# Transposed weights and attention output in one two-bank PSUM tile, four PSUM tiles for the val and proj chains

## The chip, the cores and the metric

The kernel runs on 1 core of one Trainium2 chip. Its metric is the device time of one execution in microseconds; the times below are medians of several runs.

## The reference

The reference is three steps in a row on float32 inputs (batch 8, 576 tokens, 8 heads of 64; the weights arrive as float64).

```python
scores = scale * np.matmul(q_c, k_c.transpose(0, 1, 2, 4, 3))   # chunks of 64 tokens
attn = np.exp(scores - max); attn = attn / (sum + 1e-09)
x = np.matmul(attn, v_c)                     # -> (8, 576, 512)

gate_pre[t] = sum over k of conv_w[k] * x[t - 4 + k]     # causal, 5 taps, per channel
x = (sigmoid(gate_pre) * (x @ w_val)) @ w_out

xn = (x - mu) / sqrt(var + 1e-06) * g_ln
out = x + np.maximum(xn @ w_ch1, 0.0) @ w_ch2            # 512 -> 2048 -> 512
```

## The kernel before

The kernel has two parts. The **attention stage**, up to about 344 us of the span, does the attention, the gated convolution and its two products. The **feed-forward stage** fills the rest; it starts with one block of 512 tokens in plain form (`ff1`, `ff2`: `psh`, `acc`) while the weights are still decoded (`split_ff`: VectorE's `da`, GpSimd's `w`), and goes on with pairs of blocks (`ff_pair`: `zy`, `x`, `psf`, `acc`). The change edits the attention stage alone.

The attention stage walks over 18 units of 256 tokens, one to a **slot** (`slot(u)`), and over 9 **blocks** of 512 tokens, two units each. For a unit u:

- `a3(u)`: scores. TensorE writes `sc` (two banks); VectorE takes the maximum (`mx`, line 167) and subtracts it (`ex`, line 170), ScalarE takes the exponential (line 174), VectorE the sum, the reciprocal (`sm`) and the product (`pr`, line 179).
- `a4(u)`, a slot later: eight TensorE transposes of `pr` into `pst` (line 186), which ScalarE copies to `pT` (line 188).
- `a5(u)`: TensorE multiplies `pT` by v into `x` (line 219, two banks). ScalarE copies `x` to `xf` (for the convolution) and rounds it to `xh`; VectorE makes the rest, `xl = x - xh` (line 238).

For a block j, once its two units are there:

- `conv(j, f, ...)`: per feature tile f (four of 128 channels) one ScalarE instruction (line 248) and four on VectorE (line 250), into `cg`; `sigm(j)`: one ScalarE sigmoid over all of `cg` (line 257).
- `val(j, f)`: a chain of 12 matmuls into one bank, `psv`; VectorE multiplies it by the gate (`gv`, line 282), ScalarE rounds that to `gh`, VectorE makes `gl` (line 286).
- `proj(j, t)`: per 128 tokens a chain of 12 matmuls into one bank, `pso`, over all four `gh` and `gl`; ScalarE copies it to `y` and sends it to DRAM (lines 299, 300).

The chains of a block are spread over the slots behind it, so that a slot holds its own `sc`, `pst` and `x` and four chains of earlier blocks. The first four slots are issued on TensorE in the order of the code; from slot 4 on a list scheduler sets the order on every engine by its own estimates and by which buffers it finds free, so another number of PSUM tiles gives another order. VectorE and ScalarE carry some work of the next stage as filling: the decode of the feed-forward weights of the first blocks (`da`, lines 87 to 90).

The eight PSUM banks of the stage go to four pools of two: `ps_s` for `sc`, `ps_x` for `x`, `ps_p` for `pst` (each one tile of two banks), and `ps_d` for the chains (two tiles of one bank). A chain may start when the chain two before it has been read: a `psv` by `gv`, a `pso` by `y`. Only the last block's `psv` have four tiles of their own (`acc`).

Of the kernel before, what the change touches and what calls it, by code (L numbers as in the profile page):

```python
# [8 lines left out]
F32 = mybir.dt.float32  # L9
# [5 lines left out]
PSUM = bass.MemoryType.PSUM  # L15
# [4 lines left out]
def tile_chunk_attention_gated_mlp(ctx: ExitStack, tc: tile.TileContext, qk, v, w_val, conv_w, w_out, g_ln, w1, w2, out):  # L20
    nc = tc.nc
    B, S, DM = out.shape
# [8 lines left out]
    P = 128  # L31
    BLK = 512
# [4 lines left out]
    NP = H // 2  # L37
# [10 lines left out]
    def boundary(j):  # L48
        o = (-(j * BLK)) % S
        return o if 0 < o < BLK else BLK  # L50
# [5 lines left out]
    ps_d = ctx.enter_context(tc.tile_pool(name="ps_d", bufs=2, space=PSUM))  # L56
# [4 lines left out]
    s_a = ExitStack()  # L61
    pA = s_a.enter_context(tc.tile_pool(name="pA", bufs=2, side="right"))
    ps_s = s_a.enter_context(tc.tile_pool(name="ps_s", bufs=1, space=PSUM))
    ps_x = s_a.enter_context(tc.tile_pool(name="ps_x", bufs=1, space=PSUM))
    ps_p = s_a.enter_context(tc.tile_pool(name="ps_p", bufs=1, space=PSUM))

    a_dram = [dram.tile([P, DM], F32, name=f"ad{f}") for f in range(NF)]
    w1c = [dram.tile([P, 2, 2, 2 * P], F32, name=f"wc{i}") for i in range(NF * 7 // 4)]
# [15 lines left out]
    def decode(raw, a):  # L84

        lw, hw, au = raw[:, :, 0], raw[:, :, 1], a.bitcast(U32)
        nc.scalar.activation(out=a, in_=hw.bitcast(F32), func=ACTF.Copy, scale=2.0 ** -112)
        nc.vector.tensor_scalar(out=au, in0=au, scalar1=3, scalar2=None, op0=ALU.logical_shift_left)
        nc.vector.scalar_tensor_tensor(out=au, in0=hw, scalar=0x80000000, in1=au, op0=ALU.bitwise_and, op1=ALU.bitwise_or)  # L89
        nc.vector.scalar_tensor_tensor(out=au, in0=lw, scalar=29, in1=au, op0=ALU.logical_shift_right, op1=ALU.bitwise_or)  # L90
# [55 lines left out]
    NG = NP * UN // P  # L146
# [34 lines left out]
    def a4(u):  # L181
        pr = pt.pop(u)
        t = pA.tile([P, NG, P], F32, tag="pT", name="pT", bufs=1)
        ps = ps_p.tile([P, NG, P], F32, tag="p", name="pst")
        for g in range(NG):
            nc.tensor.transpose(out=ps[:, g, :], in_=pr[:, g].rearrange("p r k -> p (r k)"), identity=ident)
        with tc.high_priority():
            nc.scalar.activation(out=t, in_=ps, func=ACTF.Copy)
            pT[u] = t
# [71 lines left out]
    def chain(ps, ops):  # L261
        n = len(ops)
        for i, (lt, rh) in enumerate(ops):
            nc.tensor.matmul(out=ps, lhsT=lt, rhs=rh, start=(i == 0), stop=(i == n - 1))  # L264

    def val(j, f):
        hs, ls = wv["vs"]
        fs = slice(f * P, (f + 1) * P)
        if j == NB - 1:
            ps = p2["acc"].tile([P, BLK], F32, tag=f"acc{f}", name="psv")  # L270
        else:
            ps = ps_d.tile([P, BLK], F32, tag="d", name="psv")
        ops = []
        for c in range(CT):
            ops += [(hs[c][:, fs], xh[j][:, c, :]), (hs[c][:, fs], xl[j][:, c, :]), (ls[c][:, fs], xh[j][:, c, :])]
        chain(ps, ops)
        o = boundary(j)
        gv = pD2.tile([P, BLK], F32, tag="gv", name="gv")
        with tc.high_priority():
            for lo, hi, sh in ((0, o, 0), (o, BLK, HALO)):  # L280
                if lo < hi:
                    nc.vector.tensor_tensor(out=gv[:, lo:hi], in0=ps[:, lo:hi], in1=cg[:, f, lo + sh:hi + sh], op=ALU.mult)  # L282
            a = pD1.tile([P, BLK], F32R, tag=f"gh{f}", name="gh")
            b = pD1.tile([P, BLK], F32R, tag=f"gl{f}", name="gl")
            nc.scalar.activation(out=a, in_=gv, func=ACTF.Copy)
            nc.vector.tensor_tensor(out=b, in0=gv, in1=a, op=ALU.subtract)  # L286
        gh[j, f], gl[j, f] = a, b

    def proj(j, t):
        hs, ls = wv["os"]  # L290
        ts = slice(t * P, (t + 1) * P)
        ps = ps_d.tile([P, DM], F32, tag="d", name="pso")
        ops = []
        for f in range(CT):
            ops += [(gh[j, f][:, ts], hs[f]), (gh[j, f][:, ts], ls[f]), (gl[j, f][:, ts], hs[f])]
        chain(ps, ops)
        y = pD2.tile([P, DM], F32, tag="y", name="y")
        with tc.high_priority():
            nc.scalar.activation(out=y, in_=ps, func=ACTF.Copy)
            nc.scalar.dma_start(out=y_dram[j][ts, :], in_=y)  # L300
# [4 lines left out]
    p2 = {}  # L305
# [67 lines left out]
    acc = {}  # L373
# [220 lines left out]
    def slot(u):  # L594
        d = [dense.get((u, i), []) for i in range(4)]
        if u + 2 < NU:
            load_qkv(u + 2)
        warm(u, 0)
        if u < NU:
            a3(u)  # L600
        warm(u, 1)
        for fn in d[0]:
            fn()
        if LAG <= u < NU + LAG:
            a4(u - LAG)
        warm(u, 2)
        for fn in d[1]:
            fn()
        if LAG <= u < NU + LAG:
            a5(u - LAG)  # L610
        warm(u, 3)
        for fn in d[2] + d[3]:
            fn()
# [30 lines left out]
    def taps():  # L644
        cwr = stg.tile([KC * CT, P], F32, tag="da", bufs=3, name="cwr")
        decode(cwu, cwr)
        ps = ps_p.tile([P, NP * P], F32, tag="p", name="pst")
        nc.tensor.transpose(out=ps[:, 0:KC * CT], in_=cwr, identity=ident[0:KC * CT, 0:KC * CT])
        nc.tensor.transpose(out=ps[:, KC * CT:(KC + 1) * CT], in_=gr, identity=ident[0:CT, 0:CT])
        nc.vector.tensor_copy(out=cw, in_=ps[:, 0:(KC + 1) * CT])  # L650
# [4 lines left out]

    at(0, 3, lambda: split_w("v"))
    at(1, 0, taps)
    at(1, 3, lambda: load_w(w_out, "o", CT))
    for c in range(CT):
        at([2, 3, 3, 4][c], [3, 0, 3, 0][c], lambda c=c: split_w("o", c, c + 1))  # L660
    for j in range(NB):
        u = UPB * (j + 1) + LAG - 1
        for f in range(CT):
            if j == NB - 1:
                at(u, 1, lambda j=j, f=f: conv(j, f, 0))
                at(u, 3, lambda j=j, f=f: conv(j, f, 1))
            elif j:
                at(*[(u, 3), (u, 3), (u + 1, 1), (u + 1, 1)][f], lambda j=j, f=f: conv(j, f, 2))
            else:
                at(u - 1, 3, lambda j=j, f=f: conv(j, f, 0))  # L670
                at(*[(u, 3), (u, 3), (u + 1, 0), (u + 1, 0)][f], lambda j=j, f=f: conv(j, f, 1))
        if j < NB - 1:
            at(u + 1, 2, lambda j=j: sigm(j))
        for f in range(CT):
            at(*[(u + 1, 2), (u + 1, 3), (u + 2, 0), (u + 2, 1)][f], lambda j=j, f=f: val(j, f))
        for t in range(BLK // P):
            at(*[(u + 2, 2), (u + 2, 3), (u + 3, 0), (u + 3, 1)][t], lambda j=j, t=t: proj(j, t))
# [123 lines left out]
```

## Time and profile before

| | |
|---|---|
| median of 3 runs | 1138.32 us (1137.65 to 1139.07) |
| the profiled execution's own time | 1135.95 us |
| its span in the trace | 1134.2 us, mean granted clock of TensorE 0.977 |
| TensorE busy | 1070.5 us |
| VectorE busy | 712.8 us |
| ScalarE busy | 483.5 us |
| GpSimd busy | 110.6 us |

A busy time is the sum over one engine's instructions. In the rows PE is TensorE's matmuls, PEld its weight loads, DVE VectorE, ACT ScalarE, POOL GpSimd, SP the queue of SyncE that issues the loads. `L264` is line 264 of the kernel before. A timeline row has start, duration, engine, line, operation, output and inputs, count, and in brackets the idle time before it with what ended it. All times are in microseconds, counted from the start of the span.

### The profile page before, as it was taken

To read this page: it belongs to the slowest core of one execution; us is meant where nothing else is said; L and a number is where in the kernel's file an instruction comes from. 1 tells how busy PE (TensorE), PEld (TensorE's weight loads), DVE (VectorE), ACT (ScalarE), POOL (GpSimd) and SP (SyncE) were. 2 spreads that over 40 slices of the span, in tenths; PEclk is the share of its full clock that TensorE was granted. 3 is DMA by queue.
4 is the path that set the end of the run, shared out by engine and by line. 5 is a ranking of instruction groups with operands and counts; after the bars stand their busy time and mean duration, and the time that the engine had idled before them with its cause. 6 is when DMAs were issued, how large, how long until landed. Compare 5 with 4: busy or idle time off the path is not lost.

```text
span 1134.2 us, 17091 instructions
## 1 busy us (share of the span) xinstructions
PE 1070.5 (94%) x6862; PEld 871.4 (77%) x6862; DVE 712.8 (63%) x1171; ACT 483.5 (43%) x832; POOL 110.6 (10%) x120
## 2 busy tenths in 40 slices
PE   5788989899898989899999999999999999999998
PEld 5676767777786868688888888888888888878877
DVE  6999999888967877545647434447444437432434
ACT  3566666566574754434444123333223333221221
POOL 2021001000003443322210000000000000000000
PEclk9799999999999999999999999999999999999999
DMA  8535546531135753634342733332733222622212
GB/s 334 169 121 166 187 133 213 179 107 72 46 120 188 225 165 119 236 118 145 126 141 100 232 99 106 112 106 89 232 105 103 99 93 89 227 93 93 75 38 75
DMA packets 58581, 155.28 MB, mean 137 GB/s; under 512 B 5742, under 2 KB 13958, under 8 KB 56198
## 3 DMA queue, kind: packets, MB, share of 16 engines
q1 hardware_dynamic: 53318, 144.75, 37.7%
q10 hardware_dynamic: 5184, 9.44, 2.2%
q8 instruction: 54, 0.88, 0.3%
q14 instruction: 25, 0.20, 0.1%
HBM read 116.41 MB, written 37.75 MB: 136 GB/s over the span
## 4 chain that ended last, share of the span: by engine, by line
PE 65%; DVE 24%; issue 4%; ACT 3%; DMA 3%; POOL 0%; SPq 0%; ACTq 0%; POOLq 0%; DVEq 0%
PE acc L499 16%; PE x L525 15%; PE psf L499 14%; PE zy L525 10%; DVE cg L250 7%; PE psv L264 5%; DVE da L89 2%; DVE da L90 2%; DVE sm L176 2%; PE acc L385 1%; DVE xl L238 1%; DMA raw<-in_moe_w_ch 1%; DVE h L537 1%; PE psh L264 1%; DVE mx L167 1%
## 5 line engine op out<-in xcount | busy, mean ns | idle before, releaser
L545 DVE TENSOR_TENSOR c<-x,c 128x512 f32<-128x512 f32 x96 | 66.2, 690 | 237.3 <-ACT c L541 181.1
L499 PE MATMUL psf<-w,h 128*128 128x512 f32 x768 | 186.0, 391 | 0.0
L499 PE MATMUL acc<-w,h 128*128 128x512 f32 x768 | 186.0, 391 | 0.0
L499 PEld LDWEIGHTS acc<-w,h 128*128 128x128 f32 x768 | 144.2, 188 | 31.4
L499 PEld LDWEIGHTS psf<-w,h 128*128 128x128 f32 x768 | 144.2, 188 | 31.4
L525 PE MATMUL x<-t,wc 128*128 128x512 f32 x576 | 148.2, 393 | 3.4 <-DVE c L545 3.4
L541 ACT ACTIVATE c<-zy 128x512 f32<-128x512 f32 x96 | 58.0, 604 | 188.4 <-PE zy L525 188.3
L525 PEld LDWEIGHTS x<-t,wc 128*128 128x128 f32 x576 | 108.8, 189 | 27.8 <-DVE c L545 4.6
L536 ACT ACTIVATE h<-c 128x512 fp32r<-128x512 f32 x96 | 60.5, 631 | 136.1 <-DVE c L545 135.5
L250 DVE SCALAR_TENSOR_TENSOR cg<-xf,cw,cg 128x516 f32<-128x516 f32 (+1 forms) x176 | 108.6, 661 | 0.0
L504 DVE TENSOR_TENSOR yt<-psf,yt 128x512 f32<-128x512 f32 x128 | 88.2, 691 | 25.0 <-PE psf L499 21.1
L525 PE MATMUL zy<-b,wc 128*128 128x512 f32 x384 | 98.9, 393 | 0.0
L525 PEld LDWEIGHTS zy<-b,wc 128*128 128x128 f32 x384 | 71.2, 188 | 14.6
L537 DVE SCALAR_TENSOR_TENSOR h<-c,h 128x512 fp32r<-128x512 f32 x96 | 68.5, 713 | 14.0 <-ACT h L536 13.9
L264 PE MATMUL psv<-xh,vh 128*128 128x512 f32 x144 | 62.1, 432 | 15.5 <-DVE gv L282 15.5
L96 POOL TENSOR_TENSOR w<-da,w 128x512 fp32r<-128x512 f32 x32 | 48.6, 1526 | 128.8 <-ACT w L95 125.6
L264 PE MATMUL psv<-xh,vl 128*128 128x512 f32 x144 | 59.6, 414 | 0.0
L264 PE MATMUL psv<-xl,vh 128*128 128x512 f32 x144 | 59.6, 414 | 0.0
L264 PE MATMUL pso<-oh,gh 128*128 128x512 f32 x144 | 58.5, 406 | 0.1
L264 PE MATMUL pso<-oh,gl 128*128 128x512 f32 x144 | 56.5, 393 | 0.4 <-DVE gl L286 0.4
L264 PE MATMUL pso<-ol,gh 128*128 128x512 f32 x144 | 56.1, 390 | 0.0
L393 POOL TENSOR_TENSOR wc<-raws,wc 128x256 fp32r<-128x256 f32 x56 | 45.3, 831 | 107.4 <-ACT wc L392 100.5
(108 smaller groups left out, 1563.3 us busy)
## 6 DMA issues: line engine op xcount, KB each, us to landing
wc<-wc SPq DMA_DIRECT2D x112, 512.0 KB, 3.2
qkr<-in_qk SPq DMA_DIRECT2D x18, 1024.0 KB, 5.9
raw<-in_moe_w_ch SPq DMA_DIRECT2D x32, 512.0 KB, 4.2
vr<-in_v SPq DMA_DIRECT2D x18, 512.0 KB, 4.2
yd<-y ACTq DMA_DIRECT2D x36, 256.0 KB, 2.8
out<-yt SPq DMA_DIRECT2D x36, 256.0 KB, 3.7
yr<-yd SPq DMA_DIRECT2D x32, 256.0 KB, 3.2
yt<-yd SPq DMA_DIRECT2D x32, 256.0 KB, 4.1
```

Source lines behind the costliest of these rows:

```text
L89: nc.vector.scalar_tensor_tensor(out=au, in0=hw, scalar=0x80000000, in1=au, op0=ALU.bitwise_and, op1=ALU.bitwise_or)
L96: nc.gpsimd.tensor_tensor(out=lo, in0=a, in1=hi, op=ALU.subtract)
L250: nc.vector.scalar_tensor_tensor(out=o, in0=x[:, f, i + lo:i + hi], scalar=cw[:, i * CT + f:i * CT + f + 1], in1=o, op0=ALU.mult, op1=ALU.add,
L264: nc.tensor.matmul(out=ps, lhsT=lt, rhs=rh, start=(i == 0), stop=(i == n - 1))
L393: eng.tensor_tensor(out=lo, in0=a, in1=hi, op=ALU.subtract)
L499: nc.tensor.matmul(out=ps, lhsT=lt, rhs=rh, start=(g == 0 and k == 0 and (first or half)), stop=(g == 1 and k == 2 and (last or half)),)
L504: nc.vector.tensor_tensor(out=yt[i], in0=ps, in1=yt[i], op=ALU.add)
L525: nc.tensor.matmul(out=ps, lhsT=lt, rhs=rh, start=(start and c == 0 and i == 0), stop=(c == 1 and i == 2), skip_group_check=True)
L536: nc.scalar.activation(out=t[:, 0, :], in_=src, func=ACTF.Relu)
L537: nc.vector.scalar_tensor_tensor(out=t[:, 1, :], in0=src, scalar=0.0, in1=t[:, 0, :], op0=ALU.max, op1=ALU.subtract)
L541: nc.scalar.activation(out=t, in_=zy, func=ACTF.Copy)
L545: nc.vector.tensor_tensor(out=t, in0=x, in1=t, op=ALU.add)
```

## The change

The pool `ps_p` is gone. The transposes `pst` go into the tile of `ps_x`, tag `x`, which `x` uses too: one tile of two banks that holds `pst` and `x` in turn. The two banks that this frees become the pool `ps_e`, two tiles of one bank, and `val` and `proj` take their tiles from `ps_d` and `ps_e` by turns as long as the stage lasts (`prep` closes it and sets `p2["acc"]`; from there on chains use `ps_d` alone). A small transpose of the convolution's taps moves from `ps_p` to `ps_e`.

```diff
-    ps_p = s_a.enter_context(tc.tile_pool(name="ps_p", bufs=1, space=PSUM))
+    ps_e = s_a.enter_context(tc.tile_pool(name="ps_e", bufs=2, space=PSUM))
...
     def a4(u):
         pr = pt.pop(u)
         t = pA.tile([P, NG, P], F32, tag="pT", name="pT", bufs=1)
-        ps = ps_p.tile([P, NG, P], F32, tag="p", name="pst")
+        ps = ps_x.tile([P, NG, P], F32, tag="x", name="pst")
...
+    chains = 0
+
+    def ps_chain(name):
+        nonlocal chains
+        chains += 1
+        pool = ps_d if chains % 2 or "acc" in p2 else ps_e
+        return pool.tile([P, BLK], F32, tag="d", name=name)
...
         else:
-            ps = ps_d.tile([P, BLK], F32, tag="d", name="psv")
+            ps = ps_chain("psv")
...
-        ps = ps_d.tile([P, DM], F32, tag="d", name="pso")
+        ps = ps_chain("pso")
...
-        ps = ps_p.tile([P, NP * P], F32, tag="p", name="pst")
+        ps = ps_e.tile([P, BLK], F32, tag="d", name="pst")
```

The scheduler gives another order. On TensorE, in the even slots of the stage's second half, where `val` chains run (here around block 5), the order before is this; the rows are the last matmuls of a block's second `psv` chain, `sc`, `pst`, and the start of its third chain:

```order
L264 MATMUL psv<-xl,vh_275 128x512
L264 MATMUL psv<-xh,vl_276 128x512
L162 MATMUL sc<-qkr 64x64 x32
L186 MATMUL pst<-ident,pr 128x128 x8
L264 MATMUL psv<-xh,vh_248 128x512
```

In the change the same place reads:

```order
L264 MATMUL psv<-xl,vh_275 128x512
L264 MATMUL psv<-xh,vl_276 128x512
L162 MATMUL sc<-qkr 64x64 x32
L264 MATMUL psv<-xh,vh_248 128x512
L264 MATMUL psv<-xl,vh_248 128x512
```

The whole third chain has moved ahead of `pst`, and the fourth stands between `pst` and `x`, where before both stood behind `pst` and ahead of `x`. The slots with `proj` chains keep their order (two chains, `sc`, a chain, `pst`, a chain, `x`).

On VectorE, at the end of block 5's convolution, the order before is this (`cg` is the convolution, `gv` the product with the gate):

```order
L179 TENSOR_TENSOR pr<-ex_144,sm 128x1024
L250 SCALAR_TENSOR_TENSOR cg<-xf,cw,cg 128x516
L238 TENSOR_TENSOR xl<-x,xh 128x4x256
L250 SCALAR_TENSOR_TENSOR cg<-xf,cw,cg 128x516
L282 TENSOR_TENSOR gv<-psv,cg 128x320 x2
```

In the change:

```order
L238 TENSOR_TENSOR xl<-x,xh 128x4x256
L250 SCALAR_TENSOR_TENSOR cg<-xf,cw,cg 128x516
L89 SCALAR_TENSOR_TENSOR da<-raw_3785,da 128x512
L250 SCALAR_TENSOR_TENSOR cg<-xf,cw,cg 128x516
L90 SCALAR_TENSOR_TENSOR da<-raw_3785,da 128x512
L88 TENSOR_SCALAR da<-da 128x512
L89 SCALAR_TENSOR_TENSOR da<-raw_3885,da 128x512
L90 SCALAR_TENSOR_TENSOR da<-raw_3885,da 128x512
L167 TENSOR_REDUCE mx<-sc 128x16
L290 TENSOR_TENSOR gv<-psv,cg 128x320 x2
```

Steps of the weights' decode, which before were all done by block 4, now reach into block 5, and `mx` of the next unit has moved ahead of `gv`. Blocks 6 and 7 have no decode steps at this place in either order.

On TensorE in the slot of the last unit, where block 7's chains run, the order before is:

```order
L264 MATMUL psv<-xl,vh_275 128x512
L264 MATMUL psv<-xh,vl_276 128x512
L186 MATMUL pst<-ident,pr 128x128 x8
L219 MATMUL x<-pT,vr 64x64 x9
L264 MATMUL psv<-xh,vh_248 128x512
L264 MATMUL psv<-xl,vh_248 128x512
```

and in the change, from the end of the third chain on:

```order
L264 MATMUL psv<-xl,vh_275 128x512
L264 MATMUL psv<-xh,vl_276 128x512
L186 MATMUL pst<-ident,pr 128x128 x8
L264 MATMUL psv<-xh,vh_248 128x512
L264 MATMUL psv<-xl,vh_248 128x512
```

Before, `pst` and the first part of `x` follow the second chain and chains 3 and 4 come behind; in the change three chains are ahead of `pst`, and the fourth is ahead of `x`.

## Rows read from the trace of the kernel before

**Rows 1.** The page: span, and busy time of each engine.

```profile
span 1134.2 us, 17091 instructions
...
PE 1070.5 (94%) x6862; PEld 871.4 (77%) x6862; DVE 712.8 (63%) x1171; ACT 483.5 (43%) x832; POOL 110.6 (10%) x120
```

**Rows 2.** Windows: stretch, its length, busy time (count) by engine, TensorE's clock, DMA share.

```profile
237.29:270.14 32.85, 30.64 (x368) 24.63 (x368) 27.78 (x41) 19.66 (x26) 0.70 (x1) 0.95 0.35 124
302.38:344.20 41.82, 41.82 (x249) 34.54 (x250) 29.30 (x69) 27.20 (x51) 0.00 (x0) 1.00 0.35 125
344.20:450.00 105.80, 98.05 (x422) 78.38 (x422) 85.48 (x147) 62.00 (x125) 45.16 (x33) 0.97 0.51 165
450.00:1134.20 684.20, 674.31 (x2971) 548.51 (x2969) 328.83 (x557) 215.14 (x422) 36.25 (x48) 1.00 0.36 123
```

**Rows 3.** TensorE's waits from 56 to 344 us: total, times, longest.

```profile
PE psv L264 <- DVE gv L282: 15.5, 6, 5.1
PE x L219 <- ACT pT L188: 9.5, 4, 3.2
```

**Rows 4.** VectorE's waits from 56 to 299.4 us.

```profile
DVE gv L282 <- PE psv L264: 11.3, 9, 2.1
DVE gv L282 <- ACT cg L257: 4.2, 3, 2.0
DVE sm L176 <- ACT ex L174: 2.4, 1, 2.4
```

**Rows 5.** Timeline of VectorE, blocks 5 and 6.

```profile
233.41 1.22 DVE L238 TENSOR_TENSOR xl<-x,xh 128x1024 fp32r<-128x1024 f32 x1
234.55 0.74 DVE L250 SCALAR_TENSOR_TENSOR cg<-xf,cw,cg 128x516 f32<-128x516 f32 x1
237.29 1.42 DVE L282 TENSOR_TENSOR gv<-psv,cg 128x320 f32<-128x320 f32 x4 [1.99 <-ACT cg L257]
...
243.08 0.76 DVE L282 TENSOR_TENSOR gv<-psv,cg 128x320 f32<-128x320 f32 x2 [0.92 <-PE psv L264]
245.97 0.76 DVE L282 TENSOR_TENSOR gv<-psv,cg 128x320 f32<-128x320 f32 x2 [2.13 <-PE psv L264]
...
253.01 0.68 DVE L238 TENSOR_TENSOR xl<-x,xh 128x512 fp32r<-128x512 f32 x1
...
270.14 1.42 DVE L282 TENSOR_TENSOR gv<-psv,cg 128x384 f32<-128x384 f32 x4 [2.00 <-ACT cg L257]
```

**Rows 6.** Timeline of TensorE, block 5.

```profile
227.42 1.16 PE L219 MATMUL x<-pT,vr 64*64 64x64 f32 x64
...
234.18 1.16 PE L162 MATMUL sc<-qkr 64*64 64x64 f32 x64
235.27 1.09 PE L186 MATMUL pst<-ident,pr 128*128 128x128 f32 x8
238.58 0.47 PE L264 MATMUL psv<-xh,vh 128*128 128x512 f32 x1 [2.22 <-DVE gv L282]
...
245.86 1.16 PE L219 MATMUL x<-pT,vr 64*64 64x64 f32 x64
```

**Rows 7.** Timeline of TensorE: the stage's last two chain matmuls.

```profile
343.56 0.39 PE L264 MATMUL pso<-ol,gh 128*128 128x512 f32 x1
343.78 0.39 PE L264 MATMUL pso<-oh,gl 128*128 128x512 f32 x1
```

**Rows 8.** The page's DMA issues: a weight load, with its time to landing.

```profile
raw<-in_moe_w_ch SPq DMA_DIRECT2D x32, 512.0 KB, 4.2
```

**Rows 9.** Groups of instructions to 480 us: busy, mean ns, idle before.

```profile
L87 ACT ACTIVATE da<-raw 128x512 f32<-128x512 f32 x40 | 26.6, 675 | 21.2 <-DMA raw<-in_moe_w_ch 8.8 <-DMA raw<-in_moe_w_val 7.5 <-POOL w L96 2.3
```

**Rows 10.** Timelines of VectorE, TensorE and GpSimd at the stage's end.

```profile
298.71 0.75 DVE L250 SCALAR_TENSOR_TENSOR cg<-xf,cw,cg 128x516 f32<-128x516 f32 x1
...
302.38 0.56 PE L219 MATMUL x<-pT,vr 64*64 64x64 f32 x18 [3.08 <-ACT pT L188]
...
346.31 1.29 POOL L96 TENSOR_TENSOR w<-da,w 128x512 fp32r<-128x512 f32 x1 [65.88 <-ACT w L95]
```

## Prediction

> **What bounds the kernel now.** I read the page's busy shares first, then the waits of each engine, then the timelines of one block of the attention stage on three engines, and last the tail of the stage. The shares [rows 1] show TensorE busy for 94% of the span and VectorE for 63%, which would make TensorE the bound everywhere. Cut into stretches the picture splits. From 450 us to the end TensorE is busy 674.31 of 684.20 us [rows 2]: nothing of this change touches that part, and it can only start sooner or later as a whole. In a block of the attention stage, here 237.29 to 270.14 us, TensorE is busy 30.64 of 32.85 us and VectorE 27.78 [rows 2]: two engines near their limit that wait for each other in turn.
>
> The waits say who waits. Between 56 and 344 us TensorE waits 15.5 us before `psv` for `gv` and 9.5 us before `x` for `pT` [rows 3]. VectorE, up to the last convolution of block 7 at 299.4 us, waits 11.3 us before `gv` for `psv`, 4.2 us before `gv` for the sigmoid (`cg`), and 2.4 us before `sm` [rows 4], with 0.5 us of small ones: 18.5 us in all.
>
> One block shows the ring that these waits form. At 234.55 VectorE does the last convolution instruction; it then waits 1.99 us for ScalarE's sigmoid, and the first two `gv` start at 237.29 [rows 5]. TensorE has finished two `psv` chains by 234.18 and may not start the third, because both chain tiles still hold products that wait for the sigmoid. It does `sc` and `pst` and stands until 238.58 [rows 6]. So VectorE then starves in turn: the third `gv` waits 0.92 us and the fourth 2.13 us for chains that TensorE began too late [rows 5]. Each engine's wait is the other's. TensorE's share of a block is 96 chain matmuls at 0.227 us from start to start [rows 7] and two each of `sc`, `pst` and `x` at 1.16, 1.09 and 1.16 us [rows 6], some 28.6 us at the full clock (its busy time of 30.64 was at a mean clock of 0.95 [rows 2]). So the block takes 32.85 us where neither needs more than about 28.6.
>
> **What the change removes.** With four chain tiles the third and fourth `psv` chain need no `gv`. In the order of the change TensorE does chain 3 right behind `sc`, and chain 4 behind `pst`. With the block's own times: `sc` ends at 235.3, chain 3 (12 x 0.227 = 2.7 us) at 238.0, `pst` at 239.0, chain 4 at 241.7, `x` at 242.9, where it ended at 247.02 before [rows 6, 7]. The third and fourth `gv` would then find their products: VectorE's 0.92 and 2.13 us fall away, and its sequence, whose order in the late blocks is nearly the same, moves up by 3.05 us. `pso` needs the fourth `gl`, which then ends near 246.0, while TensorE reaches `pso` at 242.9 and has some 4 us of products over the first two features to do; so little stands there. VectorE is then the bound, with 27.78 us of work and what it still waits for the sigmoid.
>
> Summed over the stage up to 299.4 us: all of the 11.3 us of `gv` for `psv` goes. One sigmoid wait of 1.99 us goes too, since the decodes of the first feed-forward weights (`da`) now stand between the last convolution and `gv` of block 5, where nothing stood; the wait of block 6 (2.00 us) stays [rows 5]. Of the 2.4 us before `sm`, a single wait early in the stage, I take half. Together 11.3 + 2.0 + 1.2 = 14.5 us.
>
> **What it adds.** First, every `pst` now waits until `x` of the slot before has been read by `xf`, `xh` and, last, by `xl` on VectorE. In the block shown, `xl` ends 6.05 us after `x` in the even slot (228.58 to 234.63) and 6.67 us in the odd one (247.02 to 253.69) [rows 5, 6]. Between that `x` and the next `pst`, TensorE has two chains, `sc` and a third chain to do: 5.45 + 1.16 + 2.7 = 9.3 us [rows 6, 7]. So the wait is covered by 2.6 us; with `x` 4.1 us earlier and `xl` 3.05 us earlier, by 1.5 us. If the cover is gone, TensorE stands for the excess with `pso` queued behind it, and at first only `pT` and the next `x` are late, which VectorE needs half a slot later. I cost it at nothing, with 0 to 4 us as bounds. The Trainium skill speaks against this edit: Perfetto Trace Analysis, section Optimizing Tensor Performance, wants independent matmul groups to rotate through different PSUM banks, so that the evacuation of one overlaps the next group; transposes and outputs lose that here, the chains gain it. By that rule, for the transposes alone, the sum would be that of rival 4 below, 1152 us; by the rows it is nothing, since the next group has 9.3 us of other products ahead of it.
>
> Second, block 4's decodes run later: a weight load must wait for VectorE's decode of the previous tile, and ScalarE's first step of the next decode stands in its queue ahead of two `gh`. The load takes 4.2 us to land [rows 8], then comes 0.7 us of ScalarE [rows 9] and then `gh`; VectorE has some 5 us of other work meanwhile (an estimate from the order: `mx`, four pieces of `gv`, `ex` and three decode steps). That leaves 0.7 to 1.6 us, with 0 to 4 as bounds; I take 2. Third, two engines that run this close will find small new waits; nothing before shows them. Bounds: 0, and 0.8 us a block (30.64, if TensorE's clock stays at 0.95, less 29.8 for VectorE) for eight blocks, 6.4 us. I take 1. Net up to 299.4 us: 14.5 - 2 - 1 = 11.5 us.
>
> **The tail.** From 302.38 to 344.20 us TensorE works without a gap [rows 2], so there it is the bound, and it counts how far TensorE has come when VectorE ends block 7's convolution. Before, when that convolution ends at 298.71 + 0.75, it stands; it waits 3.08 us for `pT`, which ScalarE does only after the sigmoid, up to 302.38 [rows 10], and has all of chains 3 and 4 ahead. In the change both lie before `x`. Followed through, block 7's `pso` would end about 19.5 us after the convolution instead of 21.0; then `psv` and `pso` of block 8 follow, where `gv` and `gl` come a little after the chains. I take 2.0 us more, with 0 and 5.5 us (two chains) as bounds.
>
> What follows is tied to that end: GpSimd's first `w` after the stage starts at 346.31 [rows 10], right after the last `pso` at 343.78 [rows 7], so the stretch up to 450 us moves with it, and so does the rest.
>
> **Sum.** 11.5 + 2.0 = 13.5 us. The profiled execution took 1135.95 us (span 1134.2), which gives 1122.5; the median of the runs shown, 1138.32, is 2.4 us above it, so 1138.3 - 13.5 = 1124.8 us.
>
> **The rivals.**
> 1. *The gain is half lost* (TensorE's clock stays at 0.95, or `pst` waits for `xl`, or ScalarE's queue holds `gh` back). For it: both engines need 28 to 30 us of a block, and ScalarE does `xf`, `xh` ahead of the last `gh` in the early blocks. Against it: without the stalls there is less reason for the clock to fall. It gives 13.5 - 6.4 = 7, so 1131 us.
> 2. *More is gained*: also the other sigmoid wait, all of `sm` and the full 5.5 us of the tail, and none of the new waits: 11.3 + 4.0 + 2.4 + 5.5 = 23, so 1115 us. Against it: nothing fills block 6's sigmoid wait in the new order.
> 3. *No change*: the next stage starts at its old time because its weight loads or normalisation pace it. For it: VectorE is busy 85.48 of 105.80 us there [rows 2]. Against it: `w` waits for the stage's end. 1138 us.
> 4. *Slower*: the shared tile becomes a loop of its own. It is `x` read out (6.67 us), `pst` (1.0), a chain (2.7, over `pT`), `x` (1.16), 11.6 us from one `x` to the next. A slot takes 16.4 us now. It decides once `xl` comes 4.9 us later behind `x` than now, which takes about eight convolution instructions (5.3 us) of VectorE ahead of it. Each further us costs 14 us over the 14 slots; with one, 1152 us. (The Trainium skill's rule on banks, Perfetto Trace Analysis, Optimizing Tensor Performance, points this way.) Against it: in the new order `xl` stands beside `pr`, ahead of most of them.
>
> **How the numbers follow.** Chances: forecast 0.58, rival 1 0.20, rival 2 0.10, no change 0.06, slower 0.06. The likeliest gives 1124.8, its own range 1119 to 1129. To hold 8 in 10 the range goes to 1116 (most of rival 2 left out) and 1133 (most of rival 1 taken in). About 0.2%, 2.3 us, is what a measurement of this kernel can tell from no change; faster by more holds 0.58 + 0.20 + 0.10 less a little for the weak end of rival 1: 0.87. Same 0.07, slower 0.06.
>
> **What the profile after would show.** Right: TensorE's 15.5 us before `psv` for `gv` gone or under 2; VectorE's `gv` for `psv` under 2; a block in 29.5 to 30.5 us; `x` without the waits for `pT` late in the stage; the last `pso` near 330 us, and the time from there to the end within 2 us of before. Wrong: `pst` with a wait for `xl` in most slots, `pso` waiting for `gl` by as much as `psv` did for `gv`, or a shift that is gone by 450 us.

## The result, and the profile after

The change takes 1123.63 us (median of 4 runs, 1120.93 to 1124.58) where before takes 1137.99 (median of 4 runs, 1134.46 to 1139.07): a ratio of 0.9875, 95% interval 0.9847 to 0.9903. That is 14.4 us less; the forecast was 13.5 less, 1124.8 us. The profiled execution took 1124.26 us. One run of experiment 4 below took 1319.74 us at a granted clock of 0.749, where its others had 0.98; it is left out of that row. The page of the change, beside [rows 1]:

```profile
span 1122.4 us, 17077 instructions
...
PE 1069.3 (95%) x6862; PEld 866.7 (77%) x6862; DVE 715.7 (64%) x1171; ACT 482.0 (43%) x832; POOL 108.8 (10%) x120
```

The work is the same, VectorE's even longer by 2.9 us; what went is idle time. The waits of the attention stage say which. (Line numbers in a run's rows are those of its own kernel: `gv` is line 282 before, 290 in the change, 283 in experiment 9.) TensorE after (from 56 to 344 us; total, times, longest), to be held against [rows 3]:

```profile
PE pso L264 <- DVE gl L294: 6.7, 6, 2.2
PE pso L264 <- ACT gh L293: 5.4, 6, 1.5
PE x L219 <- ACT pT L188: 0.9, 1, 0.9
```

VectorE after (56 to 300 us), to be held against [rows 4]:

```profile
DVE gv L290 <- ACT cg L257: 4.0, 2, 2.0
DVE sm L176 <- ACT ex L174: 2.3, 4, 0.7
```

`psv` no longer waits for `gv`, nor `gv` for `psv`: the ring of [rows 5, 6] is gone on both sides. No `pst` waits for `xl`. New are 12.1 us of TensorE before `pso`, for `gl` and `gh`; none of that reaches VectorE, whose list holds nothing but the sigmoid's and `sm`'s waits.

To see what this was worth, cut both traces at the same instruction, the first `gv` of block 7. Windows, before, then after (columns as in [rows 2]):

```profile
56.00:301.45 245.45, 220.54 (x2612) 176.81 (x2608) 224.78 (x334) 154.53 (x201) 21.31 (x24) 0.95 0.42 140
```

```profile
56.00:290.46 234.46, 222.51 (x2620) 175.17 (x2620) 227.85 (x333) 152.72 (x199) 19.74 (x24) 0.97 0.43 147
...
230.92:260.08 29.16, 27.52 (x357) 21.62 (x356) 26.55 (x42) 19.20 (x25) 0.46 (x1) 1.00 0.50 174
260.08:290.46 30.38, 29.48 (x316) 23.58 (x315) 27.68 (x42) 19.25 (x25) 0.32 (x1) 1.00 0.10 36
```

The stretch is 11.0 us shorter. (The work up to this mark is not quite the same: 334 and 333 VectorE instructions, 2612 and 2620 matmuls.) VectorE's idle time in it fell from 245.45 - 224.78 = 20.7 to 234.46 - 227.85 = 6.6 us, 14.1 less, and its busy time rose by 3.1. Two of the remaining waits, 4.0 of the 6.6 us, are the sigmoid's. In VectorE's timeline they stand before the first `gv` of blocks 6 and 7, and where the first feed-forward weights' decodes fill the place, in block 5, there is none:

```profile
260.08 1.42 DVE L290 TENSOR_TENSOR gv<-psv,cg 128x384 f32<-128x384 f32 x4 [2.00 <-ACT cg L257]
...
290.46 1.41 DVE L290 TENSOR_TENSOR gv<-psv,cg 128x448 f32<-128x448 f32 x4 [1.99 <-ACT cg L257]
```

The end of the stage in TensorE's timeline, beside [rows 7]:

```profile
330.65 0.39 PE L264 MATMUL pso<-oh,gl 128*128 128x512 f32 x1
330.88 2.49 PE L264 MATMUL psh<-xn,w 128*128 128x512 f32 x10
```

The first `psh` begins at 330.88, before at 344.01: 13.1 us earlier, so the stage's tail gave 2.1 us beyond the 11.0. Later the shift is 13.8 us at the first `zy` (the first product of the feed-forward stage's pairs), then 11.8 at the first `psf`, and 11.8 in the span.

### The profile page after: what moved, and what is told of

Its sections match the earlier page's. It is cut to its first block, busy times and chain, and to the rows that moved or that the text cites. A ratio compares the mean times of both kernels' runs of the same rounds, so it can differ in the third digit from the quotient of the medians.

```text
span 1122.4 us, 17077 instructions
## 1 busy us (share of the span) xinstructions
PE 1069.3 (95%) x6862; PEld 866.7 (77%) x6862; DVE 715.7 (64%) x1171; ACT 482.0 (43%) x832; POOL 108.8 (10%) x120
## 4 chain that ended last, share of the span: by engine, by line
PE 62%; DVE 27%; issue 4%; ACT 4%; DMA 2%; POOL 0%; SPq 0%; POOLq 0%; ACTq 0%; DVEq 0%
PE acc L507 15%; PE x L533 15%; PE psf L507 15%; PE zy L533 10%; DVE cg L250 8%; DVE da L90 2%; DVE da L89 2%; DVE mx L167 2%; DVE sm L176 2%; DVE xl L238 1%; PE acc L393 1%; DVE gv L290 1%; DVE pr L179 1%; DVE gl L294 1%; PE pso L264 1%
## 5 line engine op out<-in xcount | busy, mean ns | idle before, releaser
L545 DVE SCALAR_TENSOR_TENSOR h<-c,h 128x512 fp32r<-128x512 f32 x96 | 68.4, 713 | 14.1 <-ACT h L544 13.9
L264 PE MATMUL pso<-oh,gh 128*128 128x512 f32 x144 | 60.8, 423 | 5.6 <-ACT gh L293 5.4
L264 PE MATMUL psv<-xh,vh 128*128 128x512 f32 x144 | 59.1, 411 | 0.0
L264 PE MATMUL psv<-xl,vh 128*128 128x512 f32 x144 | 56.7, 393 | 0.0
L264 PE MATMUL psv<-xh,vl 128*128 128x512 f32 x144 | 56.6, 393 | 0.0
L533 PE MATMUL x<-b,wc 128*128 128x512 f32 x192 | 52.2, 408 | 4.4 <-DVE h L545 3.7
```

Of the source, the lines that this page charges most:

```text
L533: nc.tensor.matmul(out=ps, lhsT=lt, rhs=rh, start=(start and c == 0 and i == 0), stop=(c == 1 and i == 2), skip_group_check=True)
L545: nc.vector.scalar_tensor_tensor(out=t[:, 1, :], in0=src, scalar=0.0, in1=t[:, 0, :], op0=ALU.max, op1=ALU.subtract)
```

## The experiments

The table holds all kernels at the same two marks: VectorE's time from 56 us to block 7's first `gv`, and the start of the first `psh`. (Where the sigmoid is split, the gate's first product may begin before the last feature's sigmoid, so its first `gv` stands somewhat earlier in the block's work; the `psh` is free of that.) Ratios are to the kernel before in runs made beside each kernel's own; its median there was 1136.49 us for the change again, 1, 2 and 3, 1139.72 for 4, 5, 6 and the first 8, and 1137.1 for the rest, so ratios compare better than medians.

| kernel | VectorE busy + idle to block 7's `gv` | first `psh` | median us | ratio, 95% interval |
|---|---|---|---|---|
| before | 224.8 + 20.7 | 344.0 | 1137.99 | 1 |
| change | 227.9 + 6.6 | 330.9 | 1123.63 | 0.9875 [0.9847, 0.9903] |
| change again | 226.8 + 6.7 | 329.9 | 1123.09 | 0.9879 [0.985, 0.9908] |
| 1 sharing alone | 223.7 + 22.6 | 347.8 | 1137.8 | 1.001 [0.9995, 1.0026] |
| 2 four tiles, val alone | 228.0 + 7.1 | 333.5 | 1126.05 | 0.9903 [0.9872, 0.9934] |
| 3 four tiles, proj alone | 223.6 + 22.6 | 344.9 | 1137.63 | 1.0002 [0.9985, 1.002] |
| 4 three tiles | 226.8 + 8.2 | 331.9 | 1125.49 | 0.9893 [0.9864, 0.9922] |
| 5 transposes twice | 226.1 + 9.8 | 335.7 | 1125.63 | 0.9891 [0.9861, 0.9921] |
| 6 a tap less | 204.2 + 13.6 | 318.5 | 1109.21 | 0.9744 [0.9719, 0.9769] |
| 7 GpSimd less | 220.6 + 5.5 | 323.2 | 1115.58 | 0.9802 [0.9783, 0.9822] |
| 8 sigmoid in two | 225.0 + 2.5 | 327.3 | 1119.23 | 0.9841 [0.9811, 0.9871] |
| 8 again | 224.3 + 4.3 | 328.0 | 1119.54 | 0.9847 [0.9829, 0.9865] |
| 9 before, sigmoid in two | 223.7 + 2.7 | 326.3 | 1117.7 | 0.9828 [0.9813, 0.9843] |
| 10 sigmoid in four | 222.3 + 6.5 | 329.6 | 1121.69 | 0.9864 [0.9848, 0.988] |

**The change again.** The kernel of the change, unedited.

> The changed kernel once more, as it is, as the neighbour for the other runs on this chip. Ring theory (the gain is that the third and fourth val chain no longer wait for a product that VectorE reads only after the sigmoid): 1121 to 1126 us, TensorE's wait before psv for gv 0, VectorE's wait before gv for psv 0. It also tells whether the 2 us that the first profile of the change lost between 440 and 460 us, where VectorE waited 3.1 us for a row load in place of 1.5, come again (then they belong to the kernel) or not (then to that one execution).

Measured 1123.09 us, ratio 0.9879: the gain is there again, with no wait of `psv` for `gv` or of `gv` for `psv`. The longest wait for a row load between the stage's end and 480 us is 1.9 us in place of 3.1, but the stretch in which the time was lost, from the first `zy` to the first `psf`, takes 33.85 us again; so the row load alone doesn't explain it.

**1, 2 and 3: which part of the change gains.** In 1 both kinds of chain take their tiles from `ps_d`, so `pst` shares the tile of `x` and nobody gets more tiles. In 2 only `val` takes its tiles by turns, in 3 only `proj`.

```diff
1, 3:  -            ps = ps_chain("psv")
       +            ps = ps_d.tile([P, BLK], F32, tag="d", name="psv")
1, 2:  -        ps = ps_chain("pso")
       +        ps = ps_d.tile([P, DM], F32, tag="d", name="pso")
```

> Only the sharing: transposes and attention output in one two-bank tile, while val and proj keep two tiles between them, and the two freed banks stay idle. The order of instructions on TensorE and VectorE is that of the kernel before. Ring theory: no gain and next to no cost, 1136 to 1140 us; TensorE waits 15 to 17 us before psv for gv as before, and pst waits under 2 us in all for xl. Rival (the shared tile is a loop of its own): 1145 us or more, with waits before pst in most slots. Rival (the gain came from the tile layout and not from the chains): 1130 us or less.

> Sharing, and the four tiles for the val chains alone; proj takes its tiles from the first pair only. Ring theory: nearly the whole gain, 1122 to 1127 us, since the ring runs through gv and the val chains' tiles. Rival (proj needs more tiles too, because its chains wait for gl feature by feature and two open chains are not enough to fill that): 1128 to 1133 us, with 5 us or more of new waits before pso.

> Sharing, and the four tiles for the proj chains alone; val takes its tiles from the first pair only. The order of instructions on TensorE and VectorE is that of the kernel before. Ring theory: nothing, 1136 to 1140 us, with TensorE's 15 us before psv for gv still there (waits before pso were 0.4 us before). Rival (any two more tiles give half): 1129 to 1133 us.

1 and 3 have the order of before on every engine, and its time. TensorE's waits of 1, the disputed one last:

```profile
PE psv L264 <- DVE gv L290: 15.6, 6, 5.1
PE x L219 <- ACT pT L188: 8.8, 4, 3.2
...
PE pst L186 <- DVE xl L238: 0.4, 1, 0.4
```

The ring stands as before, and the shared tile costs 0.4 us of one wait. The first `psh` is 3.8 us later than before, 3.0 of it behind block 7's first `gv`. There the granted clock differs, 0.93 where the kernel before has 1.00 (302.38 to 344.20 us in [rows 2]):

```profile
302.28:347.80 45.52, 44.59 (x248) 36.57 (x249) 30.33 (x70) 28.13 (x52) 0.00 (x0) 0.93 0.32 113
```

TensorE's waits of 3:

```profile
PE psv L264 <- DVE gv L290: 13.9, 6, 3.5
```

More tiles for `proj` leave the ring alone. With 2 nearly all of the gain is there, and the waits are those of the change:

```profile
PE pso L264 <- DVE gl L294: 7.3, 7, 2.1
PE pso L264 <- ACT gh L293: 5.6, 6, 1.6
```

So it is `val`'s tiles, with the order that the scheduler finds for them. The waits before `pso` by which the rival was to be known, 5 us or more, are there, but the change with four tiles for `proj` has them as well. What `proj`'s tiles add (3.0 us by the median of the change again) lies within the overlap of the two intervals.

**4: three tiles in place of four.** `ps_e` has one tile; every third chain takes it.

```diff
-    ps_e = s_a.enter_context(tc.tile_pool(name="ps_e", bufs=2, space=PSUM))
+    ps_e = s_a.enter_context(tc.tile_pool(name="ps_e", bufs=1, space=PSUM))
...
-        pool = ps_d if chains % 2 or "acc" in p2 else ps_e
+        pool = ps_d if chains % 3 != 2 or "acc" in p2 else ps_e
```

> The change with three chain tiles in place of four, the eighth bank idle: the third val chain may start early, the fourth needs the first gv. Ring theory: most of the gain, since the first gv comes before TensorE has finished the third chain and pst: chain 4 could wait 0 to 2 us a block; 1124 to 1130 us. Rival (it takes all four, because one chain that waits holds up everything behind it on TensorE): 1132 us or more.

TensorE's waits, then VectorE's, up to block 7:

```profile
PE psv L264 <- DVE gv L290: 8.7, 6, 2.6
```

```profile
DVE gv L290 <- PE psv L264: 1.3, 2, 1.1
```

TensorE still stands 8.7 us before `psv`, more than half of before, but VectorE hardly feels it, and the time is that of the change within the intervals. More than half of TensorE's wait can stay, then, as long as VectorE's goes.

**5 and 6: which engine bounds the stage after the change.** In 5 TensorE does the eight transposes of each unit twice. In 6 VectorE leaves out the last of the five taps of the convolution, so it computes another gate.

```diff
5, in a4:
+        for g in range(NG):
+            nc.tensor.transpose(out=ps[:, g, :], in_=pr[:, g].rearrange("p r k -> p (r k)"), identity=ident)
6, in conv:
-        for i in range(1, KC):
+        for i in range(1, KC - 1):
```

> The changed kernel with every transpose of a unit done twice into the same tile: eight more TensorE instructions a slot, 18 slots at about 0.95 us, 17 us of TensorE work in all, of which some 14 lie between 56 and 300 us and 2 before. VectorE-bound theory (after the change VectorE sets the pace of the attention stage and TensorE has about 1.5 us of slack a block, 10 to 12 us in all): the time rises by 3 to 8 us against the change, 1127 to 1132 us. Rival (TensorE sets the pace): it rises by 14 to 17 us, 1138 to 1141 us.

> The changed kernel with the last of the five convolution taps left out (so the gate is another one): VectorE has four instructions of 0.66 us less a block, 2.65 us, 24 us over the nine blocks, of which 19 lie before 300 us. VectorE-bound theory: the stage shortens by most of what VectorE is ahead of TensorE, 1 to 2 us a block, 8 to 14 us in all, and then TensorE is the bound: 1110 to 1116 us. Rival (TensorE sets the pace already): 1120 us or more.

Eight transposes take 1.04 us in this row of the change's timeline:

```profile
229.57 1.04 PE L186 MATMUL pst<-ident,pr 128*128 128x128 f32 x8
```

By this row's time 18 units make 18.7 us more; from its start to that of the next chain, at 230.36, it is 0.79 us, which makes some 14 us (an estimate). The ratio, 0.9891, is the change's within the intervals, the first `psh` is 4.8 us later, and the median of 1125.63 us lies a little below the range of the VectorE-bound theory and far from the rival's: TensorE alone does not set the pace. TensorE's 12.1 us before `pso` sank to 1.7, but 7.1 us before `x` for `pT` came. The window of 5, to be held against that of the change (56.00:290.46):

```profile
56.00:291.94 235.94, 227.07 (x2787) 184.63 (x2786) 226.11 (x334) 152.87 (x197) 15.38 (x22) 0.99 0.43 146
```

TensorE's idle time fell from 12.0 us to 8.9 only. The granted clock is 0.99 in place of 0.97, and the same 896 matmuls of `sc` up to 291 us took 16.3 us in place of 19.7. So a part of the new work went into idle time, and a part was made up by the clock; how much idle time alone would have carried this run can't tell. The window of 6:

```profile
56.00:273.78 217.78, 210.88 (x2590) 170.41 (x2591) 204.19 (x298) 150.79 (x197) 18.23 (x23) 0.98 0.47 158
```

23.7 us less work on VectorE made the stretch 16.7 us shorter, and the whole 14 (1109.21 us, just below the theory's range). So VectorE is the bound, as the forecast had it, but by little: of its 23.7 us, 7.0 came back as idle time, half of it before `gv` for `psv`:

```profile
DVE gv L290 <- PE psv L264: 3.6, 6, 1.2
```

**7: where VectorE's 3.1 us more come from.** In the change some of VectorE's subtractions take nearly twice their time. Timelines of VectorE and then of GpSimd:

```profile
104.41 2.39 DVE L294 TENSOR_TENSOR gl<-gv,gh 128x512 fp32r<-128x512 f32 x2
109.24 1.28 DVE L294 TENSOR_TENSOR gl<-gv,gh 128x512 fp32r<-128x512 f32 x2
134.01 1.28 DVE L89 SCALAR_TENSOR_TENSOR da<-raw,da 128x512 uint32<-128x512 uint32 x1
136.54 0.68 DVE L90 SCALAR_TENSOR_TENSOR da<-raw,da 128x512 uint32<-128x512 uint32 x1
...
138.80 2.37 DVE L294 TENSOR_TENSOR gl<-gv,gh 128x512 fp32r<-128x512 f32 x2
...
104.37 1.28 POOL L96 TENSOR_TENSOR w<-da,w 128x512 fp32r<-128x512 f32 x1 [6.65 <-ACT w L95]
133.45 1.29 POOL L96 TENSOR_TENSOR w<-da,w 128x512 fp32r<-128x512 f32 x1 [2.33 <-ACT w L95]
139.25 1.37 POOL L96 TENSOR_TENSOR w<-da,w 128x512 fp32r<-128x512 f32 x1 [4.51 <-ACT w L95]
```

A pair of `gl` that meets GpSimd's `w` takes 2.39 or 2.37 us, one that meets none 1.28; the `da` that meets one, at 134.01, takes 1.28, the next one 0.68. The Trainium skill says why in SBUF — State Buffer, section Who interferes with whom: a VectorE instruction with two inputs in SBUF contends with a GpSimd instruction that reads SBUF, and the ports that the two engines share are an exclusive lock. This trace agrees: a pair grows by 1.1 us beside a GpSimd instruction of 1.28. In experiment 7 the eight `w` of this stretch are copied by ScalarE instead.

```diff
-        nc.gpsimd.tensor_tensor(out=lo, in0=a, in1=hi, op=ALU.subtract)
+        if low:
+            nc.gpsimd.tensor_tensor(out=lo, in0=a, in1=hi, op=ALU.subtract)
+        else:
+            nc.scalar.activation(out=lo, in_=a, func=ACTF.Copy)
...
-        a = split(t[:, 0, :], t[:, 1, :], r1, pool)
+        a = split(t[:, 0, :], t[:, 1, :], r1, pool, f >= NFA)
...
-        split(t[:, 0, :], t[:, 1, :], r2, pool)
+        split(t[:, 0, :], t[:, 1, :], r2, pool, f >= NFA)
```

> The change, with the low halves of the first eight feed-forward weight tiles copied by ScalarE in place of GpSimd's subtraction (they are then not the differences, so the output is another). In the profile of the change a pair of VectorE's gl took 2.39 us in place of 1.28 where GpSimd's w ran beside it. Theory A, that GpSimd's work beside it makes VectorE longer and VectorE is the bound: all pairs of gl near 1.28 us, VectorE busy 3 to 5 us less up to block 7's first gv, and 1117 to 1121 us. Theory B, that this time is hidden: 1122 to 1125 us. ScalarE gets eight copies of some 0.6 us more, which have room in its idle time.

Groups of VectorE to 300 us (busy, mean ns of one), of the change and then of 7:

```profile
L250 DVE SCALAR_TENSOR_TENSOR cg<-xf,cw,cg 128x516 f32<-128x516 f32 x112 | 80.9, 758 | 0.0
L294 DVE TENSOR_TENSOR gl<-gv,gh 128x512 fp32r<-128x512 f32 x31 | 23.1, 779 | 0.1
...
L89 DVE SCALAR_TENSOR_TENSOR da<-raw,da 128x512 uint32<-128x512 uint32 x13 | 10.1, 774 | 0.1
```

```profile
L253 DVE SCALAR_TENSOR_TENSOR cg<-xf,cw,cg 128x516 f32<-128x516 f32 x112 | 79.2, 746 | 0.0
L297 DVE TENSOR_TENSOR gl<-gv,gh 128x512 fp32r<-128x512 f32 x32 | 20.9, 682 | 0.6 <-ACT gh L296 0.5
```

`gl` falls from 779 to 682 ns each, the convolution from 758 to 746. VectorE's busy time up to block 7 is 220.6 us, 7.3 less than in the change and 4.2 less than before; the stretch is 8.3 us shorter and the first `psh` 7.6 us earlier. The time is 1115.58 us, below the range of theory A, which had put VectorE's gain at 3 to 5 us.

That the change pays more for such meetings than before did can be read from the traces. Take every VectorE instruction up to block 7's first `gv` that overlaps one of GpSimd in time, and count what it takes above the median of its kind without such an overlap. That sums to 4.9 us before, 8.8 in the change and 1.4 in 7. The growth of 3.9 covers the 3.1 us that VectorE's busy time rose. The order of 7 differs a little from the change's, so some tenths may be the order's.

**8, 9 and 10: the sigmoid.** The wait that is left in the change is the sigmoid's. In 8 the change gets the sigmoid in two instructions, the first three features and then the last. In 9 the kernel before gets the same, with its two chain tiles. In 10 the change gets four instructions.

```diff
8, 9:
-        nc.scalar.activation(out=cg[:, :, :n], in_=cg[:, :, :n], func=ACTF.Sigmoid)
+        for fs in (slice(0, CT - 1), slice(CT - 1, CT)):
+            nc.scalar.activation(out=cg[:, fs, :n], in_=cg[:, fs, :n], func=ACTF.Sigmoid)
10:
+        for f in range(CT):
+            nc.scalar.activation(out=cg[:, f, :n], in_=cg[:, f, :n], func=ACTF.Sigmoid)
```

> The change with the sigmoid in two instructions, three features and then the last one, so that the first gv need not wait for the convolution of the last feature. VectorE-bound theory: the two sigmoid waits of 2.0 us that are left before 300 us, and part of the 3.6 us in the tail, go: 3 to 6 us, 1118 to 1121 us. Rival (the waits move: VectorE then waits for chains, or for the exponential, behind a second sigmoid and its table load on ScalarE): 1123 us or more.

> The change with the sigmoid in two instructions once more, in more rounds: 1117 to 1121 us if the 4.4 us below the change were the sigmoid's, 1122 to 1125 us if they were the scatter of the runs.

> The kernel before, with the sigmoid of a unit in two instructions (features 0 to 2, then 3) and no other tile. Theory A, that the wait of before was a ring convolution - sigmoid - gate - val's tile - convolution, which is cut as well where the gate can begin earlier: gv's wait for psv under 6 us, and 1122 to 1132 us. Theory B, that only more tiles for the chains cut it: 1135 to 1139 us, with TensorE's wait for gv near 15 us as before.

> The change, with the sigmoid in four instructions, one for each feature. With the sigmoid in two it took 1119.23 us and showed no wait of gv for cg. Theory A, that VectorE's wait was all there was to gain: 1116 to 1121 us, the same as in two. Theory B, that each further instruction costs ScalarE's chain its start time and that the next sigmoid comes late: 1121 us or more.

8 takes 1119.23 and, again, 1119.54 us, and no `gv` waits for the sigmoid. The surprise is 9: without a tile more than before it takes 1117.7 us, below the range of its theory A, and its interval lies, barely, wholly below the change's. ScalarE's timeline in 9, where block 5's gate begins, and then VectorE's:

```profile
221.62 1.50 ACT L258 ACTIVATE cg<-cg 128x1548 f32<-128x1548 f32 x1
...
225.79 0.62 ACT L258 ACTIVATE cg<-cg 128x516 f32<-128x516 f32 x1
```

```profile
221.88 1.22 DVE L179 TENSOR_TENSOR pr<-ex,sm 128x1024 f32<-128x1024 f32 x1
223.02 1.54 DVE L250 SCALAR_TENSOR_TENSOR cg<-xf,cw,cg 128x516 f32<-128x516 f32 x2
224.47 0.75 DVE L283 TENSOR_TENSOR gv<-psv,cg 128x320 f32<-128x320 f32 x2
...
233.76 0.76 DVE L283 TENSOR_TENSOR gv<-psv,cg 128x320 f32<-128x320 f32 x2 [0.30 <-PE psv L265]
```

The first part of the sigmoid runs while VectorE still has `pr` and the last feature's taps to do; so `gv` comes without a wait, gives the two `psv` tiles back, and TensorE's third chain is in time. Of the 11.3 us of `gv` for `psv` [rows 4], 0.3 are left. The windows of 9 for the blocks up to 4, and for 5 and 6:

```profile
56.00:224.47 168.47, 156.83 (x1865) 122.93 (x1859) 168.10 (x250) 115.03 (x155) 21.45 (x21) 0.98 0.51 173
...
224.47:253.25 28.78, 28.78 (x370) 23.43 (x369) 27.84 (x43) 19.03 (x27) 0.81 (x2) 1.00 0.44 147
253.25:282.41 29.16, 29.16 (x371) 23.77 (x370) 27.77 (x43) 19.57 (x27) 0.83 (x1) 1.00 0.10 38
```

Up to block 4, where the decodes run, VectorE is busy 168.10 of 168.47 us; in blocks 5 and 6 TensorE has no gap. No wait is left there that more tiles could shorten, and 8 is no faster than 9 (1119.54 with 1118.49 to 1122.05, against 1117.7 with 1117.05 to 1118.66). In 8 the shared tile isn't free any more: one `pst` waits for `xl`.

```profile
PE pst L186 <- DVE xl L238: 1.7, 1, 1.7
```

The Trainium skill has the rule, in Perfetto Trace Analysis, section Optimizing Scalar/DVE Operations: where ScalarE or VectorE are not full but leave gaps on other engines, "breaking up instructions may allow work to be completed sooner"; 9 agrees, with 19.4 us (before took 1137.1 beside it).

10 takes 1121.69 us, in the range of theory B and 2.2 above 8, though the two overlap (1120.91 to 1123.38, and 1118.49 to 1122.05). ScalarE's groups at this line (duration min/median/max in ns, first and last start) show what four pieces bring with them:

```profile
L258 ACT ACTIVATE cg<-cg x36: 615/635/642, 55.1 to 310.5; 128x516 f32<-128x516 f32 x28, 128x512 f32<-128x512 f32 x8
L258 ACT ACT_TABLE_LOAD  x17: 1283/1283/1283, 53.8 to 308.2; - x17
```

17 table loads of 1.283 us in place of 9: between the pieces ScalarE does other functions and must come back. The exponential's line has 15 in place of 7, so ScalarE has 20.5 us more of them. In two pieces it stays at 9 and 7. That these loads make the 2.2 us is likely, not shown.

## Why the prediction was right

The time came out 1.2 us from the forecast, by the mechanism that it named: the waits of both engines at the `psv` tiles went. Part of the closeness is luck, since three of its smaller terms were wrong and one that it did not have stood in for them.

- **VectorE's `gv` for `psv`, 11.3 us, all gone:** right, none is left.
- **One sigmoid wait of 2.0 us filled by decodes, one left in block 6:** right. (The second of the 4.0 us stands in block 7, behind the stretch that [rows 4] counts.)
- **Half of the 2.4 us before `sm`:** wrong, 2.3 us remain, in four pieces in place of one.
- **`pst` behind `xl`, 0:** right. No wait in the change, 0.4 us in experiment 1, where the sharing stands alone. So rival 4, and with it the Trainium skill's rule on rotating banks (Perfetto Trace Analysis, Optimizing Tensor Performance) as a price for the transposes, does not decide here: the 9.3 us of other products cover it.
- **Block 4's weight load, 2 us, and small new waits, 1 us:** neither came. (The 2 us stood above the 0.7 to 1.6 that the forecast itself had worked out.) VectorE's waits beside the sigmoid's and `sm`'s sum to 6.6 - 4.0 - 2.3 = 0.3 us. In their place VectorE's own instructions became 3.1 us longer, because more of them meet GpSimd's `w`. The sum of 11.5 us net, measured 11.0, was right by that coincidence: 14.1 us less idle time (14.5 forecast), 3.1 us more work (3 us of waits forecast).
- **The tail, 2.0 us:** 2.1.
- **What stands before `pso`, "little":** wrong, 12.1 us, but it cost VectorE nothing.
- **A block in 29.5 to 30.5 us:** 29.16 in block 5 and 30.38 in block 6.
- **Rival 1, the clock stays at 0.95:** in blocks 5 and 6 the granted clock is 1.00, the upper level of 2.4 GHz, where block 5 had a mean of 0.95 before [rows 2]. That mean held a stretch at the lower level of 1.2 GHz, behind the 2.22 us that TensorE stood before its third chain. A window and two rows of the kernel before:

```profile
239.80:243.20 3.40, 3.40 (x9) 2.63 (x8) 2.48 (x5) 2.12 (x2) 0.00 (x0) 0.50 0.00 0
...
240.71 0.63 PE L264 MATMUL psv<-xl,vh 128*128 128x512 f32 x1
241.14 0.63 PE L264 MATMUL psv<-xh,vl 128*128 128x512 f32 x1
```

The chain's matmuls start 0.43 us apart there, in place of 0.227; the nine from 239.59 to 243.23 took 1.6 us more than nine at 0.227 (an estimate). So about half of the 3.05 us that block 5's third and fourth `gv` waited was the lower clock, which the forecast put down to the tiles alone. Both went with the stand, so the sum did not suffer.
- **Rival 3, lost by 450 us:** of 13.1 us at the stage's end 11.8 are left in the span: 0.7 more were gained up to the first `zy`, and 2.0 lost from there to the first `psf`, 33.7 us after against 31.8 before. That stretch took 33.6 us in experiment 3, which has the order of before, and 32.0 in experiment 1, so it varies without the change; why stays open.
- **The sign that was badly chosen:** "`pso` waiting for `gl` by as much as `psv` did for `gv`" was to show the forecast wrong. It nearly came (12.1 us with `gh`, against 15.5), while VectorE, which experiment 6 shows to be the bound, waited for nothing new. A wait of an engine that isn't the bound tells little; VectorE's did.

What the forecast did not see is that the ring could be cut at another place for more. It had the sigmoid in the ring, as what the two tiles wait for, but asked only for more tiles and took the sigmoid's own 2 us as a wait beside that. In experiment 9 the sigmoid's first part comes earlier and `gv` is no longer late, and with it neither are the tiles.

What stays open: how much of the gain the tiles make by themselves and how much the order that the scheduler finds with them. 2, 4, 8 and 9 all have another order than before, 1 and 3 have that of before, and no run has the new order with the old tiles and the old sigmoid. The same holds for the split sigmoid of 9, whose order on VectorE is another too. Nor is it known how much of the 11.3 us of `gv` for `psv` was the lower clock.

## What to carry to other kernels

When two engines wait for each other in turn, follow the ring through every engine before adding buffers: an extra buffer hides the late step, a smaller first piece of the late instruction brings it forward, and here the one line gave 19 us where the tiles gave 14, each with the order that came with it. Count a wait only on the engine that bounds the stage, and find out which one that is by giving each a little more or less to do. A tile that two steps of one slot can use in turn is a free source of banks where other work of the slot covers it, and only the chain that stands in the ring needs them.

## What was not expected of the hardware

A pair of VectorE's 128x512 subtractions takes 1.28 us alone and 2.37 to 2.39 us when one GpSimd subtraction of 128x512 runs at that time; without eight of these on GpSimd VectorE was busy 7.3 us less in the change (227.9 to 220.6 us). An order that removes idle time can so add busy time, without an instruction more.
